# Key projection next to the query projection, query sums head by head, and another order of the last super-chunk's products and sums

## The chip, the core and the metric

The kernel runs on one core of one Trainium2 chip. The metric is the device time of one execution in microseconds, as the median of several runs; lower is better. Five engines work side by side, each in its own fixed order: PE (TensorE: matrix products, with PEld, its loading of weights, shown as a row of its own), DVE (VectorE), ACT (ScalarE), POOL (GpSimd) and SP (SyncE, which issues the DMAs here). Engines wait for one another by semaphores.

## The reference

Linear attention with exponential features, and then a feed-forward layer with the Mish function, all in fp32:

```python
def phi(x):                                   # x: [8, 8, 576, 64]
    proj = einsum('bhsd,df->bhsf', x, w_phi)  # w_phi: [64, 128]
    proj = proj - max(abs(proj), axis=-1)
    return concatenate([exp(proj), exp(-proj)], axis=-1)
q_p, k_p = phi(q), phi(k)
kv = einsum('bhsf,bhsd->bhfd', k_p, v);  z = sum(k_p, axis=2)
attn = einsum('bhsf,bhfd->bhsd', q_p, kv) / (einsum('bhsf,bhf->bhs', q_p, z) + 1e-6)
x = attn as [4608, 512]
h = x @ w_in                                  # [512, 2048]
g = h * tanh(log1p(exp(h)))                   # Mish
out = g @ w_out                               # [2048, 512]
```

## The kernel before

**Attention** is cut into 36 units (`NU`) of 512 columns, for the keys and for the queries each. A unit holds two heads: one on partitions 0 to 63, the other on 64 to 127. For a key unit the kernel projects (`k_proj`, tile `pp_k`: 8 products with 64 rows of weights each, which the profile shows as 16 rows), takes the largest absolute value and subtracts it on DVE (`k_center`: `m_k`, then `e_k`), takes two exponentials on ACT (`k_exp`), and adds the key-value sums on PE (`k_sum`, tile `kvps`, 64 or 80 rows of the profile). For a query unit it projects (`q_proj`, `pp_q`), centres (`q_center`: `m_q`, `e_q`), transposes with TensorE in two halves, one for each head `j` (`q_turn`, tile `dt`), takes exponentials on ACT (`q_exp`), multiplies by the key-value sums (`q_num`, tile `num`, 64 rows), divides (`q_den` on ACT, `q_norm` on DVE: a reciprocal `r` and two products `x`), transposes back (`q_out`, tile `xt`) and stores to DRAM (`q_store`). The projections `pp_k` and `pp_q` share a PSUM pool of two buffers (`ps_a`); `kvps`, `dt`, `num` and `xt` share one of four (`ps_b`).

In front of the steady steps stand four key units without queries (the lead). Between the attention steps DVE, ACT and POOL also convert the feed-forward weights, a piece at a time (`weight_ops`; lines L153 to L219, tiles `w_in`, `w_out`, `t_in`, `t_out`), which are kept as a high and a low part.

**Feed-forward**: tokens are taken in super-chunks of 512 (`NSC` is 9). A step handles one super-chunk and one 256-wide piece of the 2048 hidden columns. Its products are done by Winograd's scheme for 2 by 2 blocks: seven block products `h` (`ff_in`, first 24 rows, then 18), sums on DVE (`winograd`), Mish on ACT (`mish`), and for the second half of the hidden columns another such scheme for the output: sums (`g_sums`), high and low part of the result (`g2_hi`, `g2_lo`: tiles `gh`, `gl`, `held`), and products with `w_out` in two groups: `out_now` (weights `wa`, right away, 24 products) and, after the last of four pieces of a super-chunk, `out_rest` (weights `wb`, 36 products for each `tau`, the half of the tokens). `thrice` issues the three products high x high, high x low, low x high. `drain2` takes the partial sums out of PSUM (`dp` on ACT; `du2`, `du4` and the sums into `part` on DVE; one sum on POOL) before `out_rest` may add to the same banks, and writes the output rows.

**The order of the work** is a list of events with times that are written by hand (`at(time, fn, ...)`), sorted, and issued in that order; the times are the planner's and appear nowhere on the chip. Each engine runs its instructions in that order. `K_AT`, `Q_AT`, `T_AT` and `L_AT` hold the times of the parts of key units, query units, the last four query units and the lead; `STEP2_AT` and `DRAIN_AT` those of the second feed-forward half.

Of the kernel before, what the change touches and what calls it, by code (L numbers as in the profile page):

```python
# [8 lines left out]
F32 = mybir.dt.float32  # L9
# [3 lines left out]
ALU = mybir.AluOpType  # L13
# [3 lines left out]
P = 128  # L17
# [4 lines left out]
VW = D + 1  # L22
CH = 256
# [44 lines left out]
def attention_then_mish(ctx, tc, qT, kT, va, w_phi, w_in, w_out, w_out2, out):  # L68
    nc = tc.nc
# [185 lines left out]
    def halves(ps, lhsT, rhs, start, stop):  # L255

        for h in range(2):
            rows = slice(h * D, (h + 1) * D)
            nc.tensor.matmul(ps[rows], lhsT[:, rows], rhs[h], start=start, stop=stop, skip_group_check=True)  # L259
# [75 lines left out]
    def q_num(n):  # L335
        c, g = divmod(n, 2)
        es = q_live.pop(n)
        x = x_live[n] = att.tile([P, 2, 2, P], F32, tag="x", name=f"x_{n}", bufs=3)
        for i in range(2):
            ps = ps_b.tile([P, 2, 2, VW], F32, tag="b", name=f"num{i}_{n}")  # L340
            for t in range(2):
                r0 = (2 * c + t) * P
                for j in range(2):
                    for s in range(2):
                        halves(ps[:, t, j], es[:, j, s, (2 * i + t) * P:(2 * i + t + 1) * P],
                               [kv[(r0 + h * D) // S, 2 * g + i][:, j, s] for h in range(2)],
                               start=(t == j == s == 0), stop=(s == 1))
            num_live[n, i] = ps

    def q_den(n):  # L350
        r = r_live[n] = att.tile([P, 2, 2, 2], F32, tag="r", name=f"r_{n}", bufs=3)
# [238 lines left out]
            nc.sync.dma_start(o_part[sc], part_live[s])  # L590


    def thrice(ps, gh, gl, wh, wl, start, stop):
        for k, (g, w) in enumerate(((gh, wh), (gh, wl), (gl, wh))):
            nc.tensor.matmul(ps, g, w, start=(start and k == 0), stop=(stop and k == 2), skip_group_check=True)  # L595

    def out_now(n, tau):
# [8 lines left out]
        if last:  # L606
            next_stage(s, "o", tau)
        gh, gl, wa = g_live[n]["h"], g_live[n]["l"], wout[fp][0]

        for bank, half, b in ((0, 0, 0), (0, 1, 2), (1, 0, 1), (1, 1, 3)):  # L610
            thrice(o_live[s][tau][bank][:, half], gh[:, b, cols], gl[:, b, cols], wa[:, 0, b], wa[:, 1, b],
                   first and half == 0, last)

    def out_rest(s, tau):
# [4 lines left out]
        for bank, half, gb, wb in ((0, 0, 2, 1), (1, 0, 0, 0), (1, 1, 1, 2)):  # L619
# [13 lines left out]
    def drain2(s, tau, i):  # L633
        (x, y), part = o_live[s][tau], part_blocks(s)
        if i < 3:
            assert stage[s, "o"] >= tau and stage.get((s, "d", tau), -1) == i - 1
            stage[s, "d", tau] = i
        c11, cross, c22 = part[:, 2 * tau], part[:, 2 * tau + 1:2 * tau + 5:3], part[:, 2 * tau + 5]
        if i == 0:
            p1 = ffn.tile([P, CH], F32, tag="p1", name=f"dp_{s}_{tau}", bufs=2)  # L640
            nc.scalar.copy(p1, x[:, 0])
            d_live[s, tau] = [p1]
        if i == 1:
            u2 = last_pool.tile([P, CH], F32, tag="du2", name=f"du2_{s}_{tau}", bufs=2)
            nc.vector.tensor_tensor(u2, x[:, 1], d_live[s, tau][0], op=ALU.add)  # L645
            u4 = ffn.tile([P, CH], F32, tag="u4", name=f"du4_{s}_{tau}", bufs=1)
            nc.vector.tensor_tensor(u4, y[:, 0], u2, op=ALU.add)
            nc.vector.tensor_tensor(c22, u4, c22, op=ALU.add)
            d_live[s, tau] = u2
        if i == 2:  # L650
            nc.vector.tensor_tensor(c22, y[:, 1], c22, op=ALU.add)
        if i == 3:
            nc.gpsimd.tensor_tensor(cross, cross, d_live.pop((s, tau)).unsqueeze(1).broadcast_to([P, 2, CH]), op=ALU.add)  # L653
        if i == 4:
            nc.vector.tensor_tensor(cross, y, cross, op=ALU.add)
            nc.vector.tensor_tensor(c11, x[:, 0], c11, op=ALU.add)
# [15 lines left out]
    def at(time, fn, *args):  # L672
        events.append((time, len(events), fn, args))
# [6 lines left out]
    for u in range(NU):  # L680
        t, after = base(u - LEAD), base(u - LEAD + 1)
# [199 lines left out]
```

## Time and profile before

| | |
|---|---|
| time, median of 3 runs | 1052.8 us (1051.72 to 1053.08) |
| the profiled execution | 1049.46 us, of which the span from first to last instruction is 1047.7 us |
| lead, start to the first `num` | 32.8 us |
| attention steps with keys and queries | 32.8 to 262.4 us |
| last attention units and first feed-forward steps | 262.4 to 308.6 us |
| first half of the hidden columns | 308.6 to 683 us |
| second half | 683 us to the end |
| granted TensorE clock | 1.00 in all stages |
| instructions of PE, DVE, ACT, POOL | 11848, 1158, 861, 263 |

A row of the timeline gives the start, the length of the merged run, engine, line, operation, tiles written and read, and the count; in brackets stands the idle time ahead of it and what ended it. Rows on PEld are the weight loads, whose starts follow PE's true pace; the ends of PE's own rows are modelled.

### The profile page before, as it was taken

To read this page: it belongs to the slowest core of one execution; us is meant where nothing else is said; L and a number is where in the kernel's file an instruction comes from. 1 tells how busy PE (TensorE), PEld (TensorE's weight loads), DVE (VectorE), ACT (ScalarE), POOL (GpSimd) and SP (SyncE) were. 2 spreads that over 40 slices of the span, in tenths; PEclk is the share of its full clock that TensorE was granted. 3 is DMA by queue.
4 is the path that set the end of the run, shared out by engine and by line. 5 is a ranking of instruction groups with operands and counts; after the bars stand their busy time and mean duration, and the time that the engine had idled before them with its cause. 6 is when DMAs were issued, how large, how long until landed. Compare 5 with 4: busy or idle time off the path is not lost.

```text
span 1047.7 us, 27520 instructions
## 1 busy us (share of the span) xinstructions
PE 1032.3 (99%) x11848; PEld 971.1 (93%) x11848; DVE 737.6 (70%) x1158; ACT 499.8 (48%) x861; POOL 300.0 (29%) x263
## 2 busy tenths in 40 slices
PE   8999999999999999999999999999999999999997
PEld 7899999999989999999999999999999999999997
DVE  5888788888656987486684773367667667677675
ACT  4677777777754443444443533243333333333331
POOL 0544325444620555446454540000000000000000
PEclk9999999999999999999999999999999999999999
DMA  5645646756679666664755559992451551542621
GB/s 175 203 136 176 197 141 210 279 190 223 224 228 406 236 254 228 222 231 156 280 227 192 196 177 345 386 337 93 160 201 61 183 171 72 201 146 82 216 81 41
DMA packets 87081, 208.58 MB, mean 199 GB/s; under 512 B 6960, under 2 KB 34736, under 8 KB 84144
## 3 DMA queue, kind: packets, MB, share of 16 engines
q1 hardware_dynamic: 86960, 206.83, 56.4%
q8 instruction: 93, 1.52, 0.6%
q14 instruction: 28, 0.23, 0.1%
HBM read 122.91 MB, written 83.89 MB: 197 GB/s over the span
## 4 chain that ended last, share of the span: by engine, by line
PE 97%; DMA 1%; ACT 1%; DVE 1%; issue 0%; SPq 0%; DVEq 0%; ACTq 0%
PE h L448 34%; PE o L576 19%; PE o L595 17%; PE kvps L259 7%; PE num L259 7%; PE dt L327 4%; PE pp_q L244 4%; PE pp_k L244 4%; PE xt L370 2%; DMA kraw<-kT 1%; ACT L503 0%; DVE gl L548 0%; DVE m_k L250 0%; DVE e_k L251 0%; DVE gl L517 0%
## 5 line engine op out<-in xcount | busy, mean ns | idle before, releaser
L448 PE MATMUL h<-xc,win 128*128 128x256 f32 x3024 | 381.9, 283 | 0.3 <-DVE u L476 0.3
L448 PEld LDWEIGHTS h<-xc,win 128*128 128x128 f32 x3024 | 375.3, 192 | 6.6 <-DVE u L476 0.7
L576 PE MATMUL o<-wout,gh 128*128 128x512 f32 x576 | 179.3, 392 | 0.2 <-ACT gh L511 0.2
L653 POOL TENSOR_TENSOR part<-part,du 128x512 f32<-128x512 f32 x18 | 23.3, 1295 | 389.6 <-DVE du L645 389.6
L576 PEld LDWEIGHTS o<-wout,gh 128*128 128x128 f32 x576 | 103.6, 189 | 18.4 <-ACT gh L511 0.4
L480 DVE TENSOR_TENSOR u<-h,u 128x512 f32<-128x512 f32 x72 | 49.5, 688 | 94.9 <-PE h L448 94.7
L576 PE MATMUL o<-wout,gl 128*128 128x512 f32 x288 | 112.2, 389 | 1.9 <-DVE gl L517 1.9
L595 PE MATMUL o<-wa,gh 128*128 128x256 f32 x576 | 105.3, 282 | 1.2 <-ACT gh L535 1.2
L595 PEld LDWEIGHTS o<-wa,gh 128*128 128x128 f32 x576 | 89.1, 190 | 1.4 <-ACT gh L535 1.4
L455 ACT COPY p<-h 128x256 f32<-128x256 f32 x72 | 26.4, 367 | 132.9 <-PE h L448 132.9
L333 ACT ACTIVATE e_q<-dt 128x512 f32<-128x512 f32 x144 | 77.3, 598 | 18.0 <-PE dt L327 17.8
L259 PE MATMUL kvps<-v,e_k 128*64 128x65 f32 x2560 | 83.0, 223 | 0.1
L595 PE MATMUL o<-wa,gl 128*128 128x256 f32 x288 | 81.5, 283 | 0.8 <-DVE gl L548 0.8
L259 PEld LDWEIGHTS kvps<-v,e_k 128*64 128x64 f32 x2560 | 79.2, 139 | 1.3 <-issue 0.4
L595 PE MATMUL o<-wb,held 128*128 128x256 f32 x648 | 79.2, 282 | 0.0
L595 PEld LDWEIGHTS o<-wb,held 128*128 128x128 f32 x648 | 78.4, 188 | 0.0
L259 PE MATMUL num<-kv,e_q 128*64 128x65 f32 x2304 | 74.9, 223 | 0.0
L259 PEld LDWEIGHTS num<-kv,e_q 128*64 128x64 f32 x2304 | 70.1, 137 | 4.4 <-issue 0.3
L468 DVE TENSOR_TENSOR u<-h,p 128x256 f32<-128x256 f32 x72 | 30.1, 419 | 58.4 <-ACT p L455 58.4
L576 PEld LDWEIGHTS o<-wout,gl 128*128 128x128 f32 x288 | 54.1, 188 | 14.2 <-DVE gl L517 2.5
L496 ACT ACTIVATE sb<-h 128x256 f32<-128x256 f32 x36 | 13.8, 384 | 111.8 <-PE h L448 72.8
L535 ACT CAST gh<-sb 128x1024 fp32r<-128x1024 f32 x36 | 37.8, 1051 | 40.3 <-DVE sb L528 40.3
(94 smaller groups left out, 1678.7 us busy)
## 6 DMA issues: line engine op xcount, KB each, us to landing
xc_spill<-xc SPq DMA_DIRECT2D x63, 512.0 KB, 4.6
xc<-xc_spill SPq DMA_DIRECT2D x63, 512.0 KB, 5.2
x<-x_spill SPq DMA_DIRECT2D x22, 512.0 KB, 7.0
o_part<-part SPq DMA_DIRECT2D x11, 1024.0 KB, 5.0
part<-o_part SPq DMA_DIRECT2D x11, 1024.0 KB, 5.4
in_spill<-wst_in SPq DMA_DIRECT2D x12, 896.0 KB, 4.3
win<-in_spill SPq DMA_DIRECT2D x12, 896.0 KB, 8.3
v<-va SPq DMA_DIRECT2D x32, 325.0 KB, 3.3
```

The source lines that it names most:

```text
L244: nc.tensor.matmul(ps[:, j, n], raw[rows, n * P:(n + 1) * P], w_phi2[rows], start=True, stop=True)
L259: nc.tensor.matmul(ps[rows], lhsT[:, rows], rhs[h], start=start, stop=stop, skip_group_check=True)
L327: nc.tensor.transpose(ps[:, i * P:(i + 1) * P], e[:, 0, i * P:(i + 1) * P], ident)
L333: nc.scalar.activation(e[:, s, :], ps, AF.Exp, scale=2.0 * s - 1.0)
L448: nc.tensor.matmul(ps, w, x, start=(i in (0, 2) and m == 0), stop=(m == 5), skip_group_check=True)
L455: nc.scalar.copy(p1, h_live[n][0][:, 0])
L468: nc.vector.tensor_tensor(u2, hx[:, 1], u_live[n][0], op=ALU.add)
L480: nc.vector.tensor_tensor(u[:, 0:3:2] if second(n) else u[:, 1:3], hy, u2.unsqueeze(1).broadcast_to([P, 2, CH]), op=ALU.add)
L535: nc.scalar.copy(gh, u_live[n][4])
L576: nc.tensor.matmul(ps, g, w, start=(first and f == k == 0), stop=(last and f == 1 and k == 2))
L595: nc.tensor.matmul(ps, g, w, start=(start and k == 0), stop=(stop and k == 2), skip_group_check=True)
L653: nc.gpsimd.tensor_tensor(cross, cross, d_live.pop((s, tau)).unsqueeze(1).broadcast_to([P, 2, CH]), op=ALU.add)
```

## The change

**In each attention step** the key projection is issued later (`K_AT` from -0.85 to 0.94) and the query projection's time is 1.54 instead of 0.95, so that the two stand side by side on PE, behind both halves of `dt` and behind `xt`. On PE, around the transposes of unit 2 (a name ends in the builder's own number), it was:

```order
L259 MATMUL kvps_816<-v_495,e_k_572 64x65 x8
L327 MATMUL dt_2_831<-ident,e_q_635 128x128 x4
L244 MATMUL pp_k_838<-w_phi_74,kraw_640 128x128 x8
L327 MATMUL dt_2_847<-ident,e_q_635 128x128 x4
L370 MATMUL xt_852<-ident,x_735 128x128 x4
L244 MATMUL pp_q_864<-w_phi_74,qraw_694 128x128 x8
L259 MATMUL num_2_878<-kv_364,e_q_635 64x65 x16
L259 MATMUL num_2_895<-kv_422,e_q_635 64x65 x16
```

and now, on the same engine at the same place, it is:

```order
L260 MATMUL kvps_816<-v_491,e_k_621 64x65 x8
L328 MATMUL dt_2_831<-ident,e_q_635 128x128 x4
L328 MATMUL dt_2_838<-ident,e_q_635 128x128 x4
L371 MATMUL xt_843<-ident,x_731 128x128 x4
L245 MATMUL pp_k_851<-w_phi_74,kraw_640 128x128 x8
L245 MATMUL pp_q_864<-w_phi_74,qraw_694 128x128 x8
L260 MATMUL num_2_874<-kv_353,e_q_635 64x65 x8
L260 MATMUL num_2_875<-kv_416,e_q_635 64x65 x8
L260 MATMUL num_2_874<-kv_353,e_q_635 64x65 x8
L260 MATMUL num_2_875<-kv_416,e_q_635 64x65 x8
```

The key projection has left its place between the two `dt` halves, and the score sums alternate between their two PSUM tiles: first head 0 of both, then head 1 of both. DVE, POOL and SP keep their order in this part; ACT keeps it too, but for the place of key-value copies in the lead and one copy (`p`) that changes places with `xs` at the end of attention. In the lead, the projection of key unit 4 moves from in front of the 64 sums of unit 2 to behind them.

**In the last super-chunk**, PE issues `out_now` of step 69 (weights `wa_9123`) around the last block products `h_71` in another way. Before:

```order
L595 MATMUL o_1_1_13243<-wa_9123,gh_13179 128x256 x2
L595 MATMUL o_1_1_13243<-wa_9123,gl_13185 128x256
L448 MATMUL h_71_13282<-xc_4_12873,win_9140 128x256 x6
L448 MATMUL h_71_13283<-xc_5_12877,win_9140 128x256 x6
L448 MATMUL h_71_13283<-xc_6_12900,win_9140 128x256 x6
L595 MATMUL o_0_0_13228<-wa_9194,gh_13319 128x256 x2
```

Now, on PE at the same place:

```order
L598 MATMUL o_0_1_13229<-wa_9123,gh_13179 128x256 x2
L598 MATMUL o_0_1_13229<-wa_9123,gl_13185 128x256
L449 MATMUL h_71_13282<-xc_4_12873,win_9140 128x256 x6
L449 MATMUL h_71_13283<-xc_5_12877,win_9140 128x256 x6
L449 MATMUL h_71_13283<-xc_6_12900,win_9140 128x256 x6
L598 MATMUL o_1_0_13242<-wa_9123,gh_13179 128x256 x2
```

The second half of that `out_now` (`tau` 1, 12 products into `o_1_0` and `o_1_1`) has moved behind the block products. And in `out_now` of the last step, 71, on PE, where before each pair with `gh` had its product with `gl` behind it, it is now:

```order
L598 MATMUL o_0_0_13228<-wa_9273,gh_13378 128x256 x4
L598 MATMUL o_0_1_13229<-wa_9273,gh_13378 128x256 x4
L598 MATMUL o_1_0_13242<-wa_9273,gh_13378 128x256 x4
L598 MATMUL o_1_1_13243<-wa_9273,gh_13378 128x256 x4
L598 MATMUL o_0_0_13228<-wa_9273,gl_13406 128x256 x2
L598 MATMUL o_0_1_13229<-wa_9273,gl_13406 128x256 x2
```

The 16 products with the high part come first, and the 8 with the low part last. On DVE, in all second-half super-chunks, the sum that reads PSUM (`y[:, 1]`) now stands ahead of the sum of `du4`, and in the last one the sum of the last `c11` block stands ahead of the last `cross` sums.

The diff, cut to its core:

```diff
-LEAD_STEP = 3.05
-L_AT = (0.0, 0.95, 3.4, 7.0, 9.6)
+LEAD_STEP = 3.28
+L_AT = (0.0, 0.95, 3.4, 7.0, 9.38)
...
-K_AT = (-0.85, 0.6, 3.04, 3.85, 4.24)
-Q_AT = (0.95, 3.27, 6.19, 6.49, 1.9, 3.04, 6.65, 10.0)
+K_AT = (0.94, 1.9, 3.04, 3.85, 4.24)
+Q_AT = (1.54, 3.27, 6.19, 6.49, 1.9, 3.04, 6.65, 10.0)
...
         for i in range(2):
-            ps = ps_b.tile([P, 2, 2, VW], F32, tag="b", name=f"num{i}_{n}")
-            for t in range(2):
-                r0 = (2 * c + t) * P
-                for j in range(2):
+            num_live[n, i] = ps_b.tile([P, 2, 2, VW], F32, tag="b", name=f"num{i}_{n}")
+        for j in range(2):
+            for i in range(2):
+                for t in range(2):
+                    r0 = (2 * c + t) * P
...
-    def thrice(ps, gh, gl, wh, wl, start, stop):
+    def thrice(ps, gh, gl, wh, wl, start, stop, terms=(0, 1, 2)):
         for k, (g, w) in enumerate(((gh, wh), (gh, wl), (gl, wh))):
+            if k not in terms:
+                continue
...
             nc.vector.tensor_tensor(u4, y[:, 0], u2, op=ALU.add)
-            nc.vector.tensor_tensor(c22, u4, c22, op=ALU.add)
-            d_live[s, tau] = u2
+            d_live[s, tau] = [u2, u4]
         if i == 2:
             nc.vector.tensor_tensor(c22, y[:, 1], c22, op=ALU.add)
+            nc.vector.tensor_tensor(c22, d_live[s, tau].pop(), c22, op=ALU.add)
...
         if i == 4:
             nc.vector.tensor_tensor(cross, y, cross, op=ALU.add)
+        if i == 5 or i == 4 and not (tau and s == len(segs) - 1):
             nc.vector.tensor_tensor(c11, x[:, 0], c11, op=ALU.add)
...
+            if n == len(steps) - 1:
+                a = a[:4] + tuple(x - LAST for x in a[4:])
...
             for tau in range(2):
-                at(t_of(n + 2) + 2.84, out_now, n, tau)
+                if n == len(steps) - 1:
+                    at(t_of(n + 2) + 2.84, out_now, n, tau, (0, 1))
+                else:
+                    at(t_of(n + 2) + (4.3 if n == len(steps) - 3 and tau else 2.84), out_now, n, tau)
+            if n == len(steps) - 1:
+                for tau in range(2):
+                    at(t_of(n + 2) + 2.85, out_now, n, tau, (2,))
...
-                at(t5 + 7.71, out_rest, s, 1)
+                if n == len(steps) - 1:
+                    at(t5 + 7.71, out_rest, s, 1, (0,))
+                    at(t5 + a[9] - 0.5, drain2, s, 1, 5)
+                    at(t5 + 7.71, out_rest, s, 1, (1, 2))
+                else:
+                    at(t5 + 7.71, out_rest, s, 1)
```

Some other times (`T_AT`, `JOIN`, `X0_AT`, `STEP1_AT`) change by up to 0.6 and move no instruction but the ACT copy named above.

More of the change, by code (lines that the diff above doesn't have):

```diff
@@ L32 @@
 LEAD = 4
-LEAD_STEP = 3.05
-L_AT = (0.0, 0.95, 3.4, 7.0, 9.6)
+LEAD_STEP = 3.28
+L_AT = (0.0, 0.95, 3.4, 7.0, 9.38)
 STEP = 7.43
 TAIL_STEP = 5.73
-K_AT = (-0.85, 0.6, 3.04, 3.85, 4.24)
-Q_AT = (0.95, 3.27, 6.19, 6.49, 1.9, 3.04, 6.65, 10.0)
-T_AT = (0.95, 2.0, 4.9, 5.3, 9.0, 10.38, 12.6, 13.1)
-JOIN = 1.0
+K_AT = (0.94, 1.9, 3.04, 3.85, 4.24)
+Q_AT = (1.54, 3.27, 6.19, 6.49, 1.9, 3.04, 6.65, 10.0)
+T_AT = (0.95, 2.0, 4.9, 5.3, 8.55, 10.92, 12.6, 13.1)
+JOIN = 1.22
 PRE = (11.72, 6.53)
@@ L43 @@
 WORD_AT = 4.8
-X0_AT = (37.79, 30.44)
+X0_AT = (37.79, 30.51)
 RESUME = 38.35
@@ L53 @@
 TRAIL = 8.53
-STEP1_AT = (0.75, 1.5, 1.53, 2.24, 5.7, 8.0, 6.24, 11.5, 12.4, 14.3, 18.4, 24.05)
+STEP1_AT = (0.75, 1.5, 1.53, 2.24, 5.7, 8.0, 6.24, 11.5, 12.7, 14.3, 18.4, 24.05)
 XS_AT = (1.0, 10.69, 0.03, 4.92, 1.2)
@@ L59 @@
 WB_AT = (16.0, 16.84, 19.71, 29.92)
+LAST = 1.38
 HELD_AT = (-0.43, 0.2, 0.3, 7.08)
@@ L339, in q_num @@
         for i in range(2):
-            ps = ps_b.tile([P, 2, 2, VW], F32, tag="b", name=f"num{i}_{n}")
-            for t in range(2):
-                r0 = (2 * c + t) * P
-                for j in range(2):
+            num_live[n, i] = ps_b.tile([P, 2, 2, VW], F32, tag="b", name=f"num{i}_{n}")
[3 more added lines that the diff above has]
+                    r0 = (2 * c + t) * P
                     for s in range(2):
-                        halves(ps[:, t, j], es[:, j, s, (2 * i + t) * P:(2 * i + t + 1) * P],
+                        halves(num_live[n, i][:, t, j], es[:, j, s, (2 * i + t) * P:(2 * i + t + 1) * P],
                                [kv[(r0 + h * D) // S, 2 * g + i][:, j, s] for h in range(2)],
                                start=(t == j == s == 0), stop=(s == 1))
-            num_live[n, i] = ps
     def q_den(n):
@@ L590, in drain, with out_now @@
             nc.sync.dma_start(o_part[sc], part_live[s])
-    def thrice(ps, gh, gl, wh, wl, start, stop):
+    def thrice(ps, gh, gl, wh, wl, start, stop, terms=(0, 1, 2)):
         for k, (g, w) in enumerate(((gh, wh), (gh, wl), (gl, wh))):
+            if k not in terms:
+                continue
             nc.tensor.matmul(ps, g, w, start=(start and k == 0), stop=(stop and k == 2), skip_group_check=True)
-    def out_now(n, tau):
+    def out_now(n, tau, terms=(0, 1, 2)):
         s, sc, fp, first, last = steps[n]
@@ L605, in out_now @@
         assert stage[n, "g0"] == 1
-        if last:
+        if last and 2 in terms:
             next_stage(s, "o", tau)
@@ L611, in out_now, with out_rest @@
             thrice(o_live[s][tau][bank][:, half], gh[:, b, cols], gl[:, b, cols], wa[:, 0, b], wa[:, 1, b],
-                   first and half == 0, last)
-    def out_rest(s, tau):
+                   first and half == 0, last, terms)
+    def out_rest(s, tau, parts=(0, 1, 2)):
         ns = [n for n, st in enumerate(steps) if st[0] == s]
@@ L618, in out_rest @@
         cols = slice(tau * P, (tau + 1) * P)
-        for bank, half, gb, wb in ((0, 0, 2, 1), (1, 0, 0, 0), (1, 1, 1, 2)):
+        for bank, half, gb, wb in [((0, 0, 2, 1), (1, 0, 0, 0), (1, 1, 1, 2))[i] for i in parts]:
             for n in ns:
@@ L623, in out_rest @@
                        False, n == ns[-1])
-        if tau:
+        if tau and 2 in parts:
             for n in ns:
@@ L647, in drain2 @@
             nc.vector.tensor_tensor(u4, y[:, 0], u2, op=ALU.add)
-            nc.vector.tensor_tensor(c22, u4, c22, op=ALU.add)
-            d_live[s, tau] = u2
+            d_live[s, tau] = [u2, u4]
         if i == 2:
             nc.vector.tensor_tensor(c22, y[:, 1], c22, op=ALU.add)
+            nc.vector.tensor_tensor(c22, d_live[s, tau].pop(), c22, op=ALU.add)
         if i == 3:
-            nc.gpsimd.tensor_tensor(cross, cross, d_live.pop((s, tau)).unsqueeze(1).broadcast_to([P, 2, CH]), op=ALU.add)
+            nc.gpsimd.tensor_tensor(cross, cross, d_live[s, tau][0].unsqueeze(1).broadcast_to([P, 2, CH]), op=ALU.add)
         if i == 4:
             nc.vector.tensor_tensor(cross, y, cross, op=ALU.add)
+        if i == 5 or i == 4 and not (tau and s == len(segs) - 1):
             nc.vector.tensor_tensor(c11, x[:, 0], c11, op=ALU.add)
+        if i == 4:
             for tt in (tau, 2 + tau):
```

## The prediction

> **What bounds the kernel now.** I read the page's busy times and chain of waits first, then busy times by stage, then the timeline of one attention step, then the chain of the last 30 us.
>
> ```profile
> PE 1032.3 (99%) x11848; PEld 971.1 (93%) x11848; DVE 737.6 (70%) x1158; ACT 499.8 (48%) x861; POOL 300.0 (29%) x263
> PE 97%; DMA 1%; ACT 1%; DVE 1%; issue 0%; SPq 0%; DVEq 0%; ACTq 0%
> ...
> 32.80:262.40 229.60, 229.51 (x5198) 210.35 (x5196) 193.52 (x261) 168.68 (x316) 101.67 (x92) 1.00 0.59 192
> 1028.45:1047.70 19.25, 12.31 (x99) 11.68 (x97) 9.46 (x16) 2.52 (x4) 2.59 (x2) 1.00 0.15 55
> ```
>
> The stage rows give start and end, length, then busy time of PE, PEld (weight loads), DVE, ACT, POOL, the granted clock, the DMA share and GB/s. PE sets the pace: in the 29 attention steps from 32.80 to 262.40 it is busy for 229.51 of 229.60 us. "Busy" hides something, though: the weight loader stands still for 19.25 us there. So PE can be relieved only by fewer or better-packed instructions, and the rows below show where the packing is poor. The clock is full in all stages. The last 19.25 us are different: PE works 12.31 us of them, so waits count there.
>
> One attention step, a unit's score sums (`num`) to the next unit's:
>
> ```profile
> 114.52 1.95 PEld L259 LDWEIGHTS kvps<-v,e_k 128*64 128x64 f32 x64
> 114.99 0.20 DVE L358 RECIPROCAL r<-r 128x8 f32<-128x8 f32 x1 [1.63 <-ACT r L353]
> ...
> 115.97 1.22 DVE L250 TENSOR_REDUCE m_q<-pp_q 128x8 f32<-128x1024 f32 x1
> 116.54 0.42 PEld L327 LDWEIGHTS dt<-ident,e_q 128*128 128x128 f32 x4
> 117.12 0.97 PEld L244 LDWEIGHTS pp_k<-w_phi,kraw 64*128 64x128 f32 x16 [0.17 <-issue]
> 117.22 1.23 DVE L251 TENSOR_TENSOR e_q<-pp_q,m_q 128x1024 f32<-128x1024 f32 x1
> 118.21 0.42 PEld L327 LDWEIGHTS dt<-ident,e_q 128*128 128x128 f32 x4
> 118.36 1.21 DVE L250 TENSOR_REDUCE m_k<-pp_k 128x8 f32<-128x1024 f32 x1
> 118.60 0.47 PEld L370 LDWEIGHTS xt<-ident,x 128*128 128x128 f32 x4
> 119.24 0.97 PEld L244 LDWEIGHTS pp_q<-w_phi,qraw 64*128 64x128 f32 x16 [0.17 <-issue]
> 119.61 1.22 DVE L251 TENSOR_TENSOR e_k<-pp_k,m_k 128x1024 f32<-128x1024 f32 x1
> 120.33 1.95 PEld L259 LDWEIGHTS num<-kv,e_q 128*64 128x64 f32 x64
> 120.75 0.42 DVE L158 TENSOR_SCALAR w_out<-w_out 128x512 f32<-128x512 f32 x1
> 121.20 0.43 DVE L162 TENSOR_SCALAR w_out<-w_out 128x512 uint32<-128x512 uint32 x1
> 122.67 0.20 DVE L358 RECIPROCAL r<-r 128x8 f32<-128x8 f32 x1 [1.04 <-ACT r L353]
> ```
>
> Two things are to be seen. First, each time PE goes between the projections (64 rows by 128) and the transposes (128 by 128), the loader stops: 0.17 us ahead of `pp_k` and of `pp_q`, and 0.12 us when it leaves them (117.12 + 0.97 = 118.09, next load at 118.21). Second, DVE waits in this step only ahead of `r`, so it has spare time, but not at every point of the step.
>
> **The change: key projection beside query projection.** From one start to the next, the step spends on `dt`, `pp_k`, `dt`, `xt`, `pp_q` 0.58 + 1.09 + 0.39 + 0.64 + 1.09 = 3.79 us (116.54 to 120.33). Afterwards PE does eight `dt`, then `xt`, `pp_k`, `pp_q`. Prices for these neighbours:
>
> ```profile
> 24.38 0.97 PEld L244 LDWEIGHTS pp_k<-w_phi,kraw 64*128 64x128 f32 x16
> 25.58 1.00 PEld L244 LDWEIGHTS pp_q<-w_phi,qraw 64*128 64x128 f32 x16 [0.23 <-PE pp_k L244]
> ...
> 266.76 0.86 PEld L327 LDWEIGHTS dt<-ident,e_q 128*128 128x128 f32 x8
> 267.58 0.47 PEld L370 LDWEIGHTS xt<-ident,x 128*128 128x128 f32 x4
> ```
>
> Eight `dt` in a row take 0.82 (266.76 to 267.58). `xt` in front of a projection keeps its 0.64. `pp_k` with `pp_q` behind it is the disputed one. Its 16 loads come in 8 pairs; the last load lasts 0.19, so 7 intervals fill 0.97 - 0.19 and one is 0.112, and eight are 0.90: the lower bound. The upper bound is the only place where the trace has the two beside each other, 24.38 to 25.58 = 1.20; but there `pp_q` waited 0.23, in the lead, where its input had been requested only a few us before. I take 0.90, since the pairs run evenly and the excess is named as a wait. Afterwards: 0.82 + 0.64 + 0.90 + 1.09 = 3.45, a gain of 0.34 to 0.35 a step. All 29 steps of the stage change in this way: **-10.1 us** (29 x 0.347; with the upper bound 29 x 0.05 = -1.4).
>
> [...]
>
> What hides behind PE now and is moved: `pp_k` starts later in the step. Counting from the end of `num` (114.52 here), it started 2.60 later and now starts 2.02 + 0.82 + 0.64 = 3.48 later; DVE's `m_k` follows 1.24 behind (117.12 to 118.36), at 4.72 instead of 3.84. In front of it `e_q` ends at 3.93 as before, so DVE gets a hole of 0.8. `e_k` ends at 4.72 + 2.47 = 7.19. The step, 7.68 long now (114.99 to 122.67, from `r` to `r`), becomes 7.33, and DVE should begin the next `r` at 7.33 + 0.47 = 7.80. Only 0.61 us of weight conversion fits between; what exceeds it delays `r`, `m_q` and `e_q`. PE feels this at `pp_q`, because `pp_q` writes the PSUM buffer that `e_q` of the unit before reads: slack 119.24 - 118.45 = 0.79 now, 0.44 afterwards (0.46 more where a step has 80 key sums instead of 64: 16 at 0.029). In the step above the conversions after `e_k` take 0.9 and cost nothing (0.3 late). Early in the stage there are more:
>
> ```profile
> 57.59 0.42 DVE L158 TENSOR_SCALAR w_in<-w_in 128x512 f32<-128x512 f32 x1
> 58.04 0.71 DVE L162 TENSOR_SCALAR w_in<-w_in 128x512 uint32<-128x512 uint32 x1
> 58.78 0.69 DVE L166 SCALAR_TENSOR_TENSOR w_in<-words_in,w_in 128x512 uint32<-128x512 uint32 x1
> ```
>
> 1.85 us with gaps: `r` 1.24 late, and PE waits 1.24 - 0.44 = 0.8. Done for each of the 29 steps with its own rows, five of the first ten have such a wait (0.55, 0.8, 0.35, 0.6, 0.35), two later ones 0.15 each: **+3.0 us**. Bounds: 0, if DVE catches up in the hole, and 6.9, if each of the stage's 14 weight pieces loses another 0.28 (L162 takes 0.71 here and 0.43 in the step above).
>
> What else moves: the key chain (`e_k`, two exponentials, `kvps`) starts 0.9 later but its sums come a whole step later (the next step's `kvps` is still the unit before): 0. ACT's exponentials of the second `dt` half start earlier, since the half is not behind `pp_k` any more, and the query sums head by head need that half only at their middle: 0, cover of about 1.4 us. `den` of the first tile waits for three quarters of the sums instead of half, the second tile's for the end as before: 0. SP and POOL keep their order; key loads free their buffer 0.9 later and are used three units later: 0.
>
> **The lead.** `pp_k` of unit 4 moves behind the 64 sums of unit 2, and DVE's work on it slips.
>
> ```profile
> 18.91 1.22 DVE L250 TENSOR_REDUCE m_k<-pp_k 128x8 f32<-128x1024 f32 x1 [1.09 <-PE pp_k L244]
> 30.38 1.23 DVE L251 TENSOR_TENSOR e_q<-pp_q,m_q 128x1024 f32<-128x1024 f32 x1
> ```
>
> It starts at 18.91 + 1.9 = 20.8. From there eight passes of 1.24 and 1.1 of conversions, back to back, end at 31.9 against 31.61 now, and the next `pp_q` waits for that: **+0.25 us** (bounds -0.3 and +1.0). Where attention meets the feed-forward part only one ACT pair swaps: 0 (up to +0.3). In the sums of the earlier super-chunks a 0.42 addition that frees PSUM goes ahead of the 1.09 one; PE doesn't wait there today: 0.
>
> **The end.** The first five rows are of the chain that ended last, the others of the timeline.
>
> ```profile
> 1023.69 2.17 PE h L448 x18
> 1025.89 0.70 DVE u L480
> 1028.80 1.05 ACT gh L535
> 1031.16 11.54 PE o L595 x94
> 1042.79 0.69 DVE part L655
> ...
> 1023.69 0.95 DVE L552 TENSOR_TENSOR held<-u,held 128x768 fp32r<-128x768 f32 x1
> 1029.90 0.50 PE L595 MATMUL o<-wa,gh 128*128 128x256 f32 x2 [1.17 <-ACT gh L535]
> 1031.16 0.39 PE L595 MATMUL o<-wa,gl 128*128 128x256 f32 x1 [0.76 <-DVE gl L548]
> 1031.93 0.37 ACT L641 COPY dp<-o 128x256 f32<-128x256 f32 x1 [1.35 <-PE o L595]
> 1032.34 0.42 DVE L645 TENSOR_TENSOR du<-o,dp 128x256 f32<-128x256 f32 x1 [0.36 <-ACT dp L641]
> 1033.77 8.71 PEld L595 LDWEIGHTS o<-wb,held 128*128 128x128 f32 x72
> 1043.40 0.41 DVE L656 TENSOR_TENSOR part<-o,part 128x256 f32<-128x256 f32 x1
> ```
>
> Twelve products (8.71/72 = 0.12 each, 1.44) go behind the last `h` block. DVE is held by `held` until 1024.64, so `u` starts 1.23 earlier, and so does the chain to `gh`, which ends at 1028.62 instead of 1029.85. PE, idle for 1.17 ahead of 1029.90, has then just ended its last product (1028.73) and goes on at 1028.67 without a wait worth counting; its 16 products with `gh` run to 1030.6. `gl`, which releases PE at 1031.16 now, is there at 1029.9, so the second wait of 0.76 vanishes. The 24 products end at 1031.55. The `wb` block waits until `du` has read the first bank: that bank is complete after 18 products, about 1031.1, `dp` and `du` take until 1031.97, and the block starts at 1032.0 against 1033.77: -1.77. At the very end the addition at 1043.40 moves ahead of the last `wb` products: -0.33. Together **-2.1 us** (bounds -1.2, the chain alone, and -2.6, no wait for `du`).
>
> **Sum:** -10.1 + 3.0 + 0.25 - 2.1 = -8.9 us. The profiled execution took 1049.46 us (span 1047.7 and 1.76 around it): 1040.6 for its like. The three runs' median is 1052.8, 3.3 above it; the same gain gives **1043.9 us**.
>
> **Rivals.** (1) No DVE waits: 1052.8 - 11.9 = 1040.9. For it speaks DVE's 36 us of idle time in the stage; against it, that it lies in the wrong place. 0.14. (2) Neighbouring projections are no cheaper than at 24.38: -1.4 - 2.1 + 0.25 = -3.25, 1049.6; the later `pp_q` then removes the DVE waits. For it speaks the only row; against it, the named wait and the even pairs. 0.13. (3) DVE paces the steps and eats the gain: the conversions collide with POOL. In the trace an addition with both inputs in SBUF runs 1.09 while POOL works, and 0.42 is the length of the same size from PSUM; each hit may cost 0.67. A mean delay of `r` of 0.80 makes PE wait 0.36 in each step, takes back 10.4 us against 10.1, and with -1.85 from the lead and the end leaves -1.5, 1051.3: 0.06. (4) The same mechanism on the other side: from a mean delay of 0.85 (0.44 and 0.41 of waiting: 29 x 0.41 = 11.9) the result is slower than before; at 1.0 it is 29 x (0.56 - 0.35) - 1.85 = +4.2, 1057.0. My own rows give over 0.5 only in 7 of 29 steps. 0.05. [...]
>
> **How the numbers follow.** The forecast with waits of 1 to 6.9 us, 1041.8 to 1047.8, has 0.62. The range 1040.3 to 1048.3 takes in (1) and the upper wait bound and leaves (2), (3) and (4) out, some 0.2. Three runs cannot tell less than 0.2% (2.1 us) from no change. Faster by more: 0.62 + 0.14 + 0.13 = 0.89; within: 0.06; slower: 0.05.
>
> **What would show it.** In the new trace a step of 64 key sums should take 7.33 us where DVE is not late; `pp_k` to `pp_q` 0.90 without an idle remark; `m_k` idle about 0.8 for `pp_k`; a few waits of `pp_q` for `e_q` before 110 us; the two waits near the end, for `gh` and `gl`, gone. The prediction is wrong if `pp_q` starts 1.2 behind `pp_k` throughout, if `r` never waits for ACT any more, or if `num` waits for exponentials.

## The result, and the profile after

The changed kernel takes **1042.74 us** (median of 4 runs, 1041.78 to 1043.10); the kernel before, on the same chip, 1052.94 (1051.72 to 1053.91). The ratio is 0.9905, with a 95% interval of 0.9890 to 0.9919. The forecast was 1043.9 (1040.3 to 1048.3). The change was measured twice more beside other kernels: 1041.31 against 1052.49 (ratio 0.9895, 0.9862 to 0.9927) and 1041.60 against 1053.26 (0.9895, 0.9876 to 0.9914).

The profiled execution took 1043.07 us, with a span of 1041.3. The page's busy times, and the stage rows of attention and of the end (start and end, length, then busy PE, PEld, DVE, ACT, POOL, clock, DMA share, GB/s):

```profile
PE 1023.5 (98%) x11848; PEld 970.8 (93%) x11848; DVE 732.7 (70%) x1158; ACT 497.4 (48%) x861; POOL 302.0 (29%) x263
...
32.49:257.19 224.70, 220.36 (x5199) 209.01 (x5197) 192.06 (x260) 166.76 (x318) 101.72 (x92) 1.00 0.60 198
1021.00:1041.30 20.30, 15.55 (x127) 15.06 (x125) 9.80 (x19) 3.37 (x5) 2.58 (x2) 0.99 0.14 52
```

The 29 attention steps are 4.9 us shorter (229.60 to 224.70), but PE is now idle for 4.34 us there; it was for 0.09. An ordinary step, in the timeline:

```profile
112.78 1.95 PEld L260 LDWEIGHTS kvps<-v,e_k 128*64 128x64 f32 x64
113.25 0.20 DVE L359 RECIPROCAL r<-r 128x8 f32<-128x8 f32 x1 [0.63 <-ACT r L354]
114.80 0.86 PEld L328 LDWEIGHTS dt<-ident,e_q 128*128 128x128 f32 x8
115.62 0.47 PEld L371 LDWEIGHTS xt<-ident,x 128*128 128x128 f32 x4
116.26 0.97 PEld L245 LDWEIGHTS pp_k<-w_phi,kraw 64*128 64x128 f32 x16 [0.17 <-issue]
117.14 0.98 PEld L245 LDWEIGHTS pp_q<-w_phi,qraw 64*128 64x128 f32 x16
117.47 1.23 DVE L251 TENSOR_REDUCE m_k<-pp_k 128x8 f32<-128x1024 f32 x1 [0.76 <-PE pp_k L245]
118.24 1.95 PEld L260 LDWEIGHTS num<-kv,e_q 128*64 128x64 f32 x64
```

From the first `dt` to `num` it is 114.80 to 118.24 = 3.44 us where it was 3.79; `pp_k` to `pp_q` takes 0.88 and has no idle remark; `m_k` waits 0.76 for `pp_k`. The stops of PE are elsewhere. The waits of the weight loader and of SyncE's queue between 33 and 256 us (total us, times, longest), of after and then, in two rows, of before:

```profile
PEld pp_k L245 <- issue: 4.9, 29, 0.2
PEld kvps L260 <- issue: 4.4, 3, 1.7
PEld pp_q L245 <- DVE e_q L252: 0.7, 2, 0.4
...
SPq L279 <- PE kvps L260: 96.8, 21, 8.3
```

```profile
PEld kvps L259 <- issue: 0.4, 2, 0.2
...
SPq L278 <- PE kvps L259: 98.1, 23, 8.2
```

Three pauses inside the key sums, 4.4 us together, wait for nothing that the profile shows ("issue"). Before, that row was 0.4 in all. SyncE stood at the value loads as long before as after. Of the seven waits of `pp_q` for `e_q` that were forecast, the view has two; the lengths of the steps show two more, under 0.25 us each. The end, in the timeline:

```profile
1024.49 1.23 DVE L549 TENSOR_TENSOR gl<-sb,gh 128x1024 fp32r<-128x1024 f32 x1 [0.73 <-ACT gh L536]
1024.51 2.18 PE L598 MATMUL o<-wa,gh 128*128 128x256 f32 x16
1026.53 1.12 PE L598 MATMUL o<-wa,gl 128*128 128x256 f32 x8
1027.38 0.42 DVE L648 TENSOR_TENSOR du<-o,dp 128x256 f32<-128x256 f32 x1 [0.79 <-ACT dp L644]
1027.86 8.69 PEld L598 LDWEIGHTS o<-wb,held 128*128 128x128 f32 x72 [0.41 <-DVE du L648]
1036.86 0.69 DVE L658 TENSOR_TENSOR part<-o,part 128x512 f32<-128x512 f32 x1 [2.52 <-PE o L598]
```

Both waits, for `gh` and for `gl`, are gone; the `wb` block waits 0.41 for `du`; the last addition is that of the `cross` sums. From the start of the 42 `h` products ahead of the changed part (1011.54, before 1015.62) to the end it is now 29.75 us instead of 32.06.

**Why spans and medians differ.** The spans differ by 6.4 us, the medians by 10.2. One reason stands at the entry to the feed-forward part, where PE has the same gap of 1.92 us in both (`gl` is late). The rows of the stretches behind it, of before and then of after; the share behind POOL's busy time is the granted clock:

```profile
304.00:312.00 8.00, 5.81 (x29) 4.59 (x30) 6.13 (x8) 6.58 (x11) 0.00 (x0) 1.00 0.69 229
```

```profile
303.56:306.97 3.41, 3.41 (x9) 2.65 (x10) 3.11 (x5) 1.83 (x4) 0.00 (x0) 0.50 1.05 343
```

After the gap the clock of after is halved for 3.41 us: from one group of `h` products (292.12 in after) to the next (310.14) it takes 18.02 us instead of 16.41. Before's profiled execution escaped this, and ran 3.5 under its median; 10 of the 14 executions profiled in this study did not (the last section sets the two cases side by side). The record has the mean granted clock of timed runs too. Of the 38 runs of the kernel before beside the experiments, 36 have 0.993 to 0.998 (median 0.996), and the two at 1.000 are the two fastest, 1047.96 and 1048.45. The 16 runs of the changed kernel have 0.997 to 0.999. So before's usual run loses more clock than its profiled execution shows. The old end can lose clock too (next section).

### The profile page after: what moved, and what is told of

Same layout as the page of the kernel before. It is cut to its first block, busy times and chain, and to the rows that moved or that the text cites. A ratio compares the mean times of both kernels' runs of the same rounds, so it can differ in the third digit from the quotient of the medians.

```text
span 1041.3 us, 27535 instructions
## 1 busy us (share of the span) xinstructions
PE 1023.5 (98%) x11848; PEld 970.8 (93%) x11848; DVE 732.7 (70%) x1158; ACT 497.4 (48%) x861; POOL 302.0 (29%) x263
## 3 DMA queue, kind: packets, MB, share of 16 engines
q8 instruction: 93, 1.52, 0.6%
## 4 chain that ended last, share of the span: by engine, by line
PE 97%; DVE 1%; issue 1%; ACT 1%; DMA 0%; SPq 0%; DVEq 0%
PE h L449 34%; PE o L577 19%; PE o L598 17%; PE kvps L260 7%; PE num L260 7%; PE pp_k L245 4%; PE dt L328 3%; PE pp_q L245 3%; PE xt L371 2%; DMA kraw<-kT 0%; DVE m_k L251 0%; ACT L504 0%; DVE e_k L252 0%; DVE e_q L252 0%; DVE gl L518 0%
## 5 line engine op out<-in xcount | busy, mean ns | idle before, releaser
L334 ACT ACTIVATE e_q<-dt 128x512 f32<-128x512 f32 x144 | 74.3, 604 | 6.9 <-PE dt L328 6.8
L251 DVE TENSOR_REDUCE m_k<-pp_k 128x8 f32<-128x1024 f32 x36 | 44.0, 1222 | 28.7 <-PE pp_k L245 28.7
```

The costliest lines, as they stand in the source:

```text
L251: nc.vector.tensor_reduce(m, ps, axis=AX.X, op=ALU.max, apply_absolute_value=True)
L334: nc.scalar.activation(e[:, s, :], ps, AF.Exp, scale=2.0 * s - 1.0)
```

## The experiments

Times are medians, with the ratio to the kernel before from the same chip and its 95% interval.

**1 and 2: the two halves apart.** The attention edits alone, with the last super-chunk as before:

```diff
-K_AT = (-0.85, 0.6, 3.04, 3.85, 4.24)
+K_AT = (0.94, 1.9, 3.04, 3.85, 4.24)
... (and LEAD_STEP, L_AT, Q_AT, T_AT, JOIN, X0_AT, q_num as in after)
```

> The attention edits alone, with the last super-chunk as before. Theory: the two parts add and the tail is worth the 2.3 us by which the trace shows it shorter (31.92 to 29.59), so this kernel takes 10.2 - 2.3 = 7.9 us less than before, about 1045.0. Rival: the two profiled executions speak for the timed runs as they stand; there the span up to the first row of the boundary differs by 5.2 us only (262.40 and 257.19), so 5 us less, about 1047.7. In the profile both expect steps of 7.33 and 7.79. If the three pauses of PE inside the key sums (1.63, 1.01 and 1.72 us in the profile of after) come from late instruction packets behind bunched loads, they stand in this kernel at the same steps, since its attention stage is word for word the one of after; if they are chance, at others or nowhere.

Measured: 1046.11 against 1051.88, 0.9942 (0.9929 to 0.9954): 5.8 less. And the other half, the last super-chunk's edits with these constants and sums as before:

> The last super-chunk's edits alone, with the attention of before. Theory: 2.3 us less than before, about 1050.6, from the wb block starting earlier by 1.8 and the last addition by 0.3 to 0.5. Rival: the wait for du at the head of the wb block only moves and the store sets the end, under 1 us less. The pauses of PE in the key sums should be absent or under 0.5 us in its profile, as in the profile of before, if before's profiled execution speaks for others of that order of instructions.

Measured: 1048.97, 0.9966 (0.9953 to 0.9980): 2.9 less. The parts add, within what can be told: 5.8 + 2.9 = 8.7, and 0.9942 x 0.9966 = 0.9908. Attention is worth less than the 7.9 of the theory, and the end more. The first kernel's three pauses stand in steps 9, 25 and 28 (105.32, 228.43, 251.89), as in after. The second kernel, with before's attention, missed its expectation: it has one pause of 1.06 us, at 257.77 in step 28. So pauses are not bound to the new order of the projections. In the profile of the first kernel the old end has its waits of 1.17 us for `gh` and 0.76 for `gl`, and behind them the clock is halved, as it is at the entry:

```profile
303.31:306.72 3.41, 3.41 (x10) 2.66 (x9) 3.37 (x5) 1.26 (x3) 0.00 (x0) 0.50 0.97 307
1026.93:1030.34 3.41, 3.41 (x18) 3.41 (x17) 2.57 (x6) 0.74 (x2) 1.28 (x1) 0.50 0.00 0
```

There the end takes 33.55 us, 1.5 more than in before's profiled execution. None of the 12 executions with the new end shows such a stretch while products run there. So the end's edits save the clock loss where there was one, and besides, against before's profiled end, 2.3 us in eight of these twelve profiles and 1.4 to 1.7 in the other four, where the time behind the last product is 0.6 longer.

**3: the order of the query sums.**

```diff
-        for j in range(2):
-            for i in range(2):
-                for t in range(2):
-                    r0 = (2 * c + t) * P
...
+            for t in range(2):
+                r0 = (2 * c + t) * P
+                for j in range(2):
...
```

> After, with the query sums in the old order (bank by bank, the two heads in turn). Theory: the order is worth nothing in most steps, since in the profile of after the last exponential ends 0.69 us ahead of the first sum in 20 of 35 steps and 0.2 us behind it in two; the second head is then needed 0.23 instead of 0.93 us into the sums, which costs 0 to 0.7 us in all: 1042.7 to 1043.4. Rival: the head-by-head order carries a part of the gain (each sum waits for ScalarE in many steps), 2 us more than after or over.

Measured: 1041.52, 0.9903 (0.9887 to 0.9919), the same as after within these bounds. Head by head or not is worth nothing that the runs can tell.

**4: the pauses; value loads later.**

```diff
-        at(t - 0.8 * STEP, v_load, u)
+        at(t + (0.15 if u >= LEAD else -0.8) * STEP, v_load, u)
```

> After, with the value loads issued about 7 us later from the fifth on, so that SyncE's queue no longer stands at them for the key sums of three pairs before (96.8 us of waits in the profile of after, up to 8.3) and the loads behind them aren't let go in bunches of five. Theory: a 16 KB packet of PE's instructions waits behind those bunches; the three pauses (4.4 us) were packets that ended over 1.7 blocks of 256 instructions into PE's stream, where others end at 0.9 to 1.6. With the bunches spread they go: 1038 to 1040, and no pause over 0.5 us inside the key sums. Rival: the pauses are late values (the load and not the instructions); then a later load makes them longer, 1043 or more. Second rival: chance of one execution, and the timed runs don't have them: 1042.7.

Measured: 1039.72, 0.9886 (0.9869 to 0.9903), 3.0 under the first result of after. The DMA of after in two neighbouring stretches, the first up to the packet ahead of the first pause (busy tenths of the 16 DMA engines in 40 slices; then for each queue its packets, MB and share of the engines' time):

```profile
DMA  0000039593499879698779979999999999842222
...
q1 hardware_dynamic: 710, 1.63, 73.8%
```

```profile
q8 instruction: 1, 0.02, 5.9%
q1 hardware_dynamic: 6, 0.01, 3.1%
```

The first is 97.0 to 103.9 us: five loads and stores were let go within 2 us when SyncE's wait at a value load ended, and in 6.9 us queue q8 gets no packet through. The second is 103.9 to 104.9: one packet. Queue q8, which the profile calls "instruction", holds 93 packets of 16 KB, 1.52 MB in all. Shared out over PE's 23,696 products and loads that is 64 bytes each and 255 to a packet, an estimate that takes them all for PE's instructions; one packet comes in some 5.5 us in this stage. The key sums beside it:

```profile
103.20 1.42 PEld L260 LDWEIGHTS kvps<-v,e_k 128*64 128x64 f32 x45
106.26 0.34 PEld L260 LDWEIGHTS kvps<-v,e_k 128*64 128x64 f32 x8 [1.63 <-issue]
```

PE stops in the middle of one tile's sums and goes on 1.41 us after the packet's end (104.85). In the kernel with later value loads the same stretch, 97.0 to 103.9, and the waits:

```profile
q1 hardware_dynamic: 490, 0.96, 47.3%
q8 instruction: 1, 0.02, 1.2%
...
SPq L379 <- ACT xs L378: 100.7, 26, 6.7
SPq L279 <- PE kvps L260: 12.3, 9, 5.4
...
PEld kvps L260 <- issue: 0.6, 1, 0.6
```

The packet passes among the loads, SyncE's wait at the value loads falls from 96.8 to 12.3 us (its time at other rows grows), and one pause of 0.6 us is left of 4.4. The late-values rival is out: later values did not make the pauses longer.

**5, 6: the waits of `pp_q`; conversions into the hole ahead of `m_k`.** The sixth run has the value loads of experiment 4 as well. (`quiet` marks the second half of the weights, which keeps its times.)

```diff
-        ops = [(0.0, absolute), (0.9, clamp), (1.35, shift), (1.8, sign), (2.5, scale)]
+        ops = [(0.0, absolute), (0.9, clamp), (1.35, shift), (7.43, sign), (7.93, scale)] if not quiet else [(0.0, absolute), (0.9, clamp), (1.35, shift), (1.8, sign), (2.5, scale)]
...
-        at(clock - 12.0, weight_load, *pc)
+        at(clock - (12.0 if quiet else 16.0), weight_load, *pc)
...
-            at(clock - WORD_AT + delay, op)
+            at(clock - (WORD_AT if quiet else 9.2) + delay, op)
```

> After, with the four weight conversions on VectorE moved: two stand between e_q and m_k of one step, two between e_q and m_k of the next, none behind e_k or r (their words are loaded 4 us earlier). Theory: the waits of pp_q for e_q (0.41, 0.51, 0.09 and 0.22 us in the profile of after) come from conversions ahead of r, which push e_q back; with the conversions in the hole of 0.76 to 1.23 us ahead of m_k they go, 1.2 us less than after: about 1041.5. Rival: the hole is not free (e_k becomes late and the key exponentials with it), 0 to 3 us more than after. The pauses in the key sums can change by their own share, up to 4 us either way, since the word loads move; the profile separates the two.

Measured: 1043.36, 0.9898 (0.9867 to 0.9928): no gain over after (1041.31 in the same session).

> After, with both the value loads issued later and the conversions moved. Theory: the two gains add: value loads 3.0 (1039.72 against 1042.74), conversions 1.2, about 1038.5, with no wait of pp_q over 0.2 us and no pause over 0.7 us in the key sums. Rival: the earlier word loads bunch with others again and bring the pauses back, 1041 to 1043.

Measured: 1042.70, 0.9896 (0.9870 to 0.9923): the gain of the value loads is gone again, though not by pauses: none stands in its key sums. The theory fell; the sixth kernel's profile shows why (timeline, and the waits of the loader):

```profile
69.28 2.09 POOL L211 TENSOR_TENSOR win<-w_in,win 128x896 fp32r<-128x896 f32 x1 [1.35 <-ACT win L207]
69.41 2.25 DVE L163 TENSOR_SCALAR w_in<-w_in 128x512 uint32<-128x512 uint32 x1
71.58 1.21 DVE L251 TENSOR_REDUCE m_k<-pp_k 128x8 f32<-128x1024 f32 x1
76.54 0.42 PEld L371 LDWEIGHTS xt<-ident,x 128*128 128x128 f32 x4 [0.59 <-ACT kv L309]
...
PEld xt L371 <- ACT kv L309: 3.3, 5, 0.8
PEld pp_q L245 <- DVE e_q L252: 0.3, 2, 0.2
```

The waits of `pp_q` did shrink from 0.7 to 0.3. But this conversion began 0.13 us behind POOL's long difference and ended 0.29 us after it (71.37 and 71.66): 2.25 us for what takes 0.43 where POOL is not ahead of it. Of the 16 conversions of this kind in this stage, seven took 2.25 to 2.32 us, each begun just behind that difference on POOL; the fifth kernel has seven as well, after none over 0.8. `m_k` is late, ACT's key exponentials too, then its copy of `kv`, and `xt` waits for that copy's buffer, 3.3 us in five steps. Why the conversion lasts past POOL's instruction was not shown.

**7: the neighbours undone.**

```diff
-K_AT = (0.94, 1.9, 3.04, 3.85, 4.24)
+K_AT = (-0.785, 1.9, 3.04, 3.85, 4.24)
```

> After, with the key projection between the query transposes and the transposes of x: all the rest as in after, but one change of matmul shape more in each step, as in before. Theory by the count of changes: the pair costs 0.347 us as between before and after, 29 times, 10.1 us more than after: 1052 to 1053. Theory by the rows of the blocks themselves: the eight query transposes stay together (0.82), so only pp_k goes from 0.90 to 1.09, 29 x 0.19 = 5.5 us more: about 1048. Rival: the gain came from something else that moved with the projection (e_k's place on VectorE, the shorter sums), then 1043 to 1044.

Measured: 1048.31, 0.9957 (0.9940 to 0.9975), 7.0 more than after in the same session. By the time alone the second theory (about 1048) would have won; the profile decides otherwise. Its timeline, one step:

```profile
114.57 0.86 PEld L328 LDWEIGHTS dt<-ident,e_q 128*128 128x128 f32 x8
115.59 0.97 PEld L245 LDWEIGHTS pp_k<-w_phi,kraw 64*128 64x128 f32 x16 [0.17 <-issue]
116.69 0.42 PEld L371 LDWEIGHTS xt<-ident,x 128*128 128x128 f32 x4
117.27 0.97 PEld L245 LDWEIGHTS pp_q<-w_phi,qraw 64*128 64x128 f32 x16 [0.17 <-issue]
118.37 1.95 PEld L260 LDWEIGHTS num<-kv,e_q 128*64 128x64 f32 x64
```

114.57 to 118.37 is 3.80, against 3.44 in after and 3.79 in before, and its steps are 7.68 and 8.14 long, those of before. So the count of changes decides, not which blocks stand beside each other: `dt` with a projection behind it takes 1.02 for eight, not 0.82, since the stop of 0.17 ahead of the projection comes on top. In 29 steps that is 10.0 us. That only 7.0 of it shows in the time (6.2 between the two profiled executions, 1047.70 and 1041.46) has two reasons in the profiles: the lead is 1.06 shorter here (`num` at 31.26 instead of 32.32, since the fifth key projection stands elsewhere), and waits and pauses above the bare step lengths are 1.9 us instead of 4.7.

**8 and 12: after again.**

> After, unchanged, for comparison on the same chip. By the result 1042.7, a ratio of 0.9905 to before. Theory on the pauses (instruction packets behind bunched loads): PE stands again in the key sums of the same steps, 9, 25 and 28, by 0 to 2 us each, as the packet comes. Theory of chance: at other steps, or none.

Measured: 1041.31. The pauses of over 0.3 us in the key sums stand at 52.1, 229.0 and 251.2 us, in steps 2, 25 and 28 (1.24, 0.76, 0.35): step 2 in place of the expected 9.

> After, unchanged, beside the three others. By the result and its repetition 1041 to 1043, with 1 to 5 us of pauses in the key sums. Theory of instruction packets: where a pause stands, the packet that ended last ahead of it did so over 1.6 blocks into PE's stream.

Measured: 1041.60; pauses at 52.5, 106.9, 230.1 and 252.3, in steps 2, 9, 25 and 28 (1.78, 0.69, 1.41, 0.35). The places return and the sizes vary. Two rows of it, and one of the eleventh kernel:

```profile
52.51 1.36 PEld L260 LDWEIGHTS kvps<-v,e_k 128*64 128x64 f32 x44 [1.78 <-issue]
230.12 0.13 PEld L260 LDWEIGHTS kvps<-v,e_k 128*64 128x64 f32 x1 [1.41 <-issue]
```

```profile
250.35 0.78 PEld L260 LDWEIGHTS kvps<-v,e_k 128*64 128x64 f32 x24 [1.14 <-issue]
```

The last packets on q8 ahead of them ended at 50.98, 228.70 and 248.82: 1.53, 1.42 and 1.53 before PE went on. Over all profiles 25 pauses of 0.35 to 2.82 us stand in key sums between 33 and 256 us, in ten executions, and two more just behind, in two of the three with before's step lengths (1.06 in experiment 2, 0.47 at 257.04 in 7). Every one of the 27 ends 1.20 to 1.58 us after the end of such a packet, and packets come only every 5.3 to 5.7 us on average. The "1.6 blocks" of the expectation were too sharp: at 256 records to a block (16 KB at the 64 bytes estimated above), the packets ahead of the 25 ended 1.46 to 1.75 blocks into PE's stream, but eleven others at 1.55 to 1.66 caused no pause of 0.3 us or more; some records are missing from the count. The longest pauses cost more than their length: behind those of 2.15 us in experiment 3 and 2.82 in 5 the clock was halved for 3.41 us, and their steps took 11.23 and 11.85 us where 7.33 is usual.

**9: the stream shifted by half a packet.**

```diff
     make_identity(nc, ident)
+    scrap = ps_b.tile([P, 512], F32, tag="b", name="scrap")
+    for _ in range(64):
+        nc.tensor.matmul(scrap[0:32, 0:2], ident[:, 0:32], ident[:, 0:2], start=True, stop=True)
```

> After, with 64 small matmuls (128 instructions, half a 16 KB block) ahead of the first projection, where PE waits for the first keys anyway; their result is not used. Theory of instruction packets: each packet is now asked for half a block, some 2.7 us, earlier against the loads, so the packet that ran into the bunch of five loads at step 9 (issued 97.1 to 98.9 in the profile of after) goes ahead of it or has time left: the pauses at steps 9, 25 and 28 (1.63, 1.01, 1.72 us) do not stand there again together; others may stand at other steps, always where a packet ends over 1.6 blocks into PE's stream. Time 1039 to 1043. Theory of data (late values, or SBUF traffic): the loads and the order of the work are the same, so the pauses stay in the same steps.

Measured: 1045.61, 0.9932 (0.9915 to 0.9950). Two misses. The added products were not free: the first `num` stands at 37.1 instead of 32.2 to 32.5, and the clock is halved once more on the way (15.09 to 18.50 us). And the pauses answer to neither theory cleanly: gone at step 28, under 0.3 at step 25, new at step 7 (0.39), but still there at steps 2 and 9 (0.83, 1.16). A bunch like that of 97 to 105 us lasts longer than the 5.5 us between packets, so it catches one packet at any phase. This run does not tell the theories apart; experiment 4 and the 1.2 to 1.6 us behind the packets do.

**10 and 11: a faster kernel, and its base.**

```diff
+        ops = [(0.0, absolute), (0.9, clamp), (1.35, shift), (1.8, sign), (2.5, scale)] if quiet else [(0.0, absolute), (0.86, clamp), (1.0, shift), (3.2, sign), (3.7, scale)]
...
+        at(t + (0.15 if u >= LEAD else -0.8) * STEP, v_load, u)
+        at(t + (-0.785 if u == LEAD else a[0]), k_proj, u)
...
+        word_at = clock - WORD_AT if quiet else CONV[0] - WORD_AT + 2 * STEP * i
```

The eleventh run has the `v_load` line alone, and is the kernel of experiment 4 again; the tenth has all of it.

> The kernel with the value loads issued later, unchanged, beside after on the same chip. By the first comparison 1039.7, 2 to 3 us less than after, with SyncE's wait at the value loads near 12 us instead of 97 and no pause over 0.7 us in the key sums. Rival: the difference was that of two chips or of chance, within 1 us of after.

Measured: 1040.06 (1037.86 to 1040.53), 0.9873 (0.9852 to 0.9894), beside after's 1041.60 (1040.60 to 1044.44): 1.5 less by medians, 2 to 3 forecast, and all its runs lie under all of after's. No pause over 0.7 was expected, but two of 1.2 and 1.1 us are left; ahead of the first, from 162 to 170 us, ten transfers stand close together without a wait for values.

> After, with three edits: value loads issued later (as before, alone 3.0 less by the first comparison); the fifth key projection, the first after the lead, where the kernel with the projection between the transposes had it (its first query sum began at 31.26 instead of 32.3 to 32.5: 1.1 us less); the conversions of VectorE at a fixed place, two behind e_k in one step, two between e_q and m_k in the next, since the pair between e_q and m_k of the first step ran into the weight difference on POOL (2.25 us for an instruction of 0.42). Theory: against the kernel with the value loads alone 1.1 + 0.7 us less (the waits of pp_q, 0.7 in its profile), about 1037.9. Rival: the lead's gain is used up by a wait of the first steps for VectorE, and the conversions between e_q and m_k collide again: 1040 or more, with waits of xt for the copy of kv as the sign.

Measured: **1038.27** (1038.04 to 1038.82), 0.9861 (0.9841 to 0.9881): the fastest here, 3.3 under after. In its profile nothing waits for VectorE or for `kv` in this stage; one pause of 1.17 remains. The first `num` is at 31.96, so of the 1.1 us of the lead 0.2 to 0.5 came.

## Why the prediction was right, point by point

The time was inside the range and 1.2 us under the forecast. Terms, in us, from the profiled executions:

| term | predicted | measured |
|---|---|---|
| neighbours, 29 steps | -10.1 | -10.06 (steps of 7.33 and 7.795 for 7.68 and 8.14) |
| waits of `pp_q` for VectorE | +3.0 | +0.7 in the view of waits, +1.25 by the step lengths (four steps) |
| pauses for instructions, odd waits | none | +4.8, where before has 0.9 |
| lead | +0.25 | -0.3 (+0.1 to -0.2 against experiment 2, with before's lead) |
| from the end of the attention steps to the 42 `h` products ahead of the end | 0 | +1.15 (the halved clock +1.6) |
| end | -2.1 | -2.3 (-1.4 to -2.3 over the profiles), and up to 1.5 more where the clock had fallen |

- **Neighbours: right, and shown** by undoing them alone (experiment 7). The lower bound for `pp_k`, 0.90, was the right one of the two; 24.38 to 25.58 had been a wait.
- **VectorE's waits: mechanism right, size off.** The hole of 0.8 ahead of `m_k` came (0.76), and `pp_q` waits for `e_q` in the two steps where three conversions stand behind `e_k` (0.41 and 0.51 us), and a little in two of those with two (0.09 and 0.22); forecast were seven such waits. The delay of `r` was carried from step to step too strictly.
- **Missed: the instruction pauses.** I costed what moved at nothing because SyncE's order of loads stayed the same, and took "issue" for a property of shape changes alone. The runs show PE waiting 0.35 to 2.82 us for instruction packets held up by bunched loads. The attention edits alone have three such pauses; before's profiled execution has none over 0.3, and the two others with its step lengths have one each (1.06 and 0.47). The loads stood as bunched before (SyncE's wait 98.1 and 96.8 us), so the bunching alone does not say why the shorter steps meet it more often; that stays open.
- **The lead: within its bounds, but not understood.** The first `num` stands at 32.2 to 32.5 in after's three profiles, and at 32.43 and 32.80 in the two with before's lead. With the projection of unit 4 ahead of the sums it stands at 31.26 (experiment 7) and 31.96 (experiment 10). So the move seems to cost 0.2 to 1.2 us, and something else in the lead's edits to win it back; what that is was not tested.
- **The end: right.** The `wb` block, counted from the 42 `h` products, starts 1.84 earlier (1.77 predicted), with 0.41 of waiting for `du` (0.45). Not foreseen was the halved clock behind the two waits (3.41 us in the first kernel, 1.5 us of time), which no profile with the new end shows.
- **That the sum came so close was luck.** Between the two profiled executions the gain is 6.4 us, not 8.9. The forecast took 1.75 to 2.3 too much for VectorE, 3.9 too little for the pauses, and nothing for the clock at the entry (1.6). The medians are nearer because before's usual run loses clock that its profiled execution did not lose: the forecast added 3.3 us for the usual run and called its gain the same. The granted clocks of the timed runs bear this out (0.996 in the median before, 0.998 after); where a timed run lost it, they do not tell.
- **The rivals.** (1), no waits, came nearest to what VectorE does; (2) fell with `pp_k` to `pp_q` at 0.88; (3) and (4) did not happen in after, but what they rest on, VectorE held up while POOL works, appeared once conversions were moved (2.25 to 2.32 us for what took 0.43, in experiments 5 and 6).

## What to carry to other kernels

Count the changes of matmul shape on TensorE in a loop body and put products of one shape side by side: here a pair of changes was worth 0.35 us a pass, in both arrangements that were tried. Where PE stops in the middle of a run of products and the profile says "issue", look at the instruction queue among the DMA packets and at what SyncE lets go at once; here value loads that waited for their buffer, 96.8 us in all, held those behind them, and five loads and stores went out within 2 us. So issue such a load when its buffer is free: that left 12.3 and 9.5 us of the wait in two runs (experiments 4 and 11), and 0.6 and 2.3 of 4.4 us of pauses. And before comparing two spans, look at the granted clock behind idle time of PE that adds up to about 2 us: before's profiled execution was spared the halved clock that 10 of the 14 show behind the 1.92 us at the entry.

## What the runs showed of the hardware

- **Packets of the instruction queue came late behind bunched loads, and PE stood still.** PE goes on 1.20 to 1.58 us after the end of a 16 KB packet, in all 27 pauses; in after's own three it is 1.41, 1.35 and 1.27. Three such pauses took 4.4 us of after's attention stage.
- **Where PE was idle for 1.86 us or more within one window of 3.41 us, the clock was halved in the next.** In after the granted clock changes at 13.43, 303.56, 306.97 and 1040.84 us, 85, 1 and 215 times 3.413 us apart, and in every profile here the changes lie whole multiples of 3.413 us apart; in the first kernel's rows above the two halved stretches start 723.62 us apart, 212 times that. Cut into windows on that grid, from 20 us to the end of the products, the 14 profiles have 13 windows in which PE is idle for 1.86 us or more in all, and a halved window follows each; in the other 4144 it is idle for 1.78 us or less, and none follows (idle time from PE's rows, gaps of 0.3 us and more). The gap at the entry is 1.92 us in all 14 profiles. In ten it falls into one window with at least 1.86 us, and costs some 1.6 us more: in after it stands from 301.48 to 303.40, in the window from 300.15 to 303.56. In four the border of two windows divides it, and it costs nothing more: in before 0.30 us of it lie ahead of the border at 307.00 and 1.62 behind. In the first kernel's end the waits of 1.17 and 0.76 us add up to 1.93 in one window.
